# A parallel Hedgehog-attention and gMLP block: a later GELU, sixteen loads of wo, remainders split in place, and block stores on GpSimd's queue

## The chip, the core and the metric

The kernel runs on one core of one Trainium2 chip. The metric is device time in microseconds (us), median of three runs; beside it there is one profiled execution, whose trace gives the time of every instruction on TensorE (PE, with its weight loads as PEld), VectorE (DVE), ScalarE (ACT), GpSimd (POOL) and SyncE (SP, which here only issues DMAs). SPq, POOLq and ACTq are the queues of these engines.

## The reference

x has 2048 tokens of 512 features. After one layer norm, two branches are added to x: linear attention with a learned double softmax over 32 heads, and a gMLP whose spatial gate mixes all 2048 tokens.

```python
xn = _layernorm(x, axis=-1)
return x + _A_ref(xn, A_wqkv, A_w_phi, A_wo) + _B_ref(xn, B_w_in, B_w_sp, B_b_sp, B_w_out)

# attention branch: feature map, sums over tokens, projection by wo
phi_q = concat(softmax(pq), softmax(-pq));  phi_k = concat(softmax(pk), softmax(-pk))
kv = einsum("bhsf,bhsd->bhfd", phi_k, v);   z = einsum("bhsf->bhf", phi_k)
o = einsum("bhqf,bhfd->bhqd", phi_q, kv) / (einsum("bhqf,bhf->bhq", phi_q, z)[..., None] + 1e-6)
return o.transpose(...).reshape(B, S, D) @ wo

# gMLP branch: 688 + 688 features, spatial product over tokens
z = gelu(x @ w_in);  z1 = z[..., :Fh];  z2 = layernorm(z[..., Fh:])
g = einsum("ts,bsf->btf", w_sp, z2) + b_sp[None, :, None]
return (z1 * g) @ w_out
```

All matrices are float32.

## The kernel before

Tokens are cut into 16 tiles of 128 rows. A float32 product is made of three TensorE products of rounded parts: a matrix is split into its rounded part and the rest, by a copy on ACT (`round_h`, L45) and a subtraction on DVE (`rest_l`, L49), and `mm3` (L51) multiplies high by high, high by low and low by high.

The program has four stages. From 0 to about 225 us the tokens are normalised, turned and projected; z1 (the first 688 features of the gMLP, before GELU) and the attention's exponentials go out to DRAM (`z1_d`, `e_d`). From there to about 290 us z2 is projected, normalised and split into the operands B. Then comes the **spatial stage**, to about 506 us, and last the **output stage**, which multiplies the gated tiles by w_out and the attention's output by wo and adds x.

The spatial stage works on pairs of token tiles, i = 0 to 7 (`NP` is 8). For a pair, `products` runs over four groups of source tokens (`NQ` is 4; n counts the 32 groups of the stage). One group is 7 block products (`FORM`, a form of Strassen's) of 6 matmuls, so a pair is 168 matmuls into seven PSUM tiles g. Two groups ahead, `prep_a` makes the operands A for group n + 2: sums S on DVE, and for each of four pieces a rounding on ACT and a subtraction on DVE. `load_a` loads the raw weights `wf` three groups ahead on SP's queue.

At the end of a pair, `drain` adds up the seven PSUM tiles into the tile c (first the ACT copy of L711, then seven DVE additions, L710 to L715), and `gate` does the rest: GELU on ACT over `z1t`, the product of GELU and c on DVE (L727), the split of the 48 remainder columns into a rounded part and a rest (L730, L49, L732; 688 is five times 128 plus 48), and a transpose in blocks of 32 on DVE (L733), which writes its result **back into `z1t`**. Four stores then carry `z1t` to `u_d` in DRAM, 32 partitions each, in runs of 32 elements (128 bytes): 32 x 46 = 1472 runs a store. `z1t` and `c` have one buffer each, so the next pair's `load_z1` (two loads on POOL's queue) waits until the four stores have landed, and GELU waits for that load. Before, the stores stand on SP's queue among the loads of `wf`; those of pair 6 are held back behind the loads `et`.

A scheduler turns program order into the order of each engine. It places instructions by an estimate of its own; `tc.issue_after(ins)` ties those inside it behind `ins` on the same engine. `gate` ties GELU behind the first drain copy. Within an engine the order is then fixed: whoever waits holds up all behind it.

In the output stage, tiles u come back from `u_d` (`fetch_u`: five blocks u and the 96 remainder rows rt), are split, and are multiplied by w_out (`project_u`). `attend_T` and `attend` turn the attention's features and multiply them by kv into the tile po; oT is its split form, and `project_o` multiplies oT by wo. wo itself is loaded at the start of this stage: four loads of 128 rows, whose source pattern takes 32 rows from each of four places, each followed by a split into woh and wol. The tiles er are copies of finished features made by DMA on POOL's queue. The gate of pair 7 runs in the middle of this stage (after tile 8), with its own stores from `zt`.

Of the kernel before, what the change touches and what calls it, by code (L numbers as in the profile page):

```python
# [10 lines left out]
F32 = mybir.dt.float32  # L11
F32R = mybir.dt.float32r
# [6 lines left out]
P = 128  # L19
S, D, H, DH, FH = 2048, 512, 32, 16, 688  # L20
# [4 lines left out]
NF = 2 * D  # L25
KF = FH // P
REM = FH - KF * P
FU = FH + REM
BL = 32
# [3 lines left out]
NP = NT // 2  # L33
HP, QP = P // 2, P // 4
# [3 lines left out]
def mixer(ctx: ExitStack, tc: tile.TileContext, x, x_t, wv, wqkT, phi_bd, wo, w_in, wst, b_r, w_out, out):  # L38
    nc = tc.nc
    pe, act, dve, pool, sp = nc.tensor, nc.scalar, nc.vector, nc.gpsimd, nc.sync  # L40


    def round_h(eng, h, src):
        if eng is act:
            return act.activation(h, src, AF.Copy).ins  # L45
        return eng.tensor_copy(h, src).ins

    def rest_l(l, src, h, eng=None):
        return (eng or dve).tensor_tensor(l, src, h.bitcast(F32), op=ALU.subtract).ins  # L49
# [19 lines left out]
    e_d = dram.tile([NT, P, NF + 2 * H], F32, name="e_d")  # L69
# [96 lines left out]
    with ExitStack() as p0:  # L166
# [71 lines left out]
        xt, v, rounded, ready = {}, {}, [], []  # L238
# [131 lines left out]
        t = xz.tile([P, 2, FH], F32R, tag="xz", name="xT")  # L370
        xT.append(t)
        x0, pts = xt.pop(0), []
        for k in range(2):
            pts.append(ps.tile([P, 2, P], F32, tag="mm", name="pt"))
            for c in range(2):
                i = pe.transpose(pts[k][:, c], x0[:, (2 * k + c) * P:(2 * k + c + 1) * P], ident).ins
            keep(pe=i)
        warm_up(2)
        for cs, pt in zip(halves, pts):
            src = pt.rearrange("p a b -> p (a b)")  # L380
            i = round_h(act, t[:, 0, cs], src)
# [7 lines left out]
        p = ps.tile([P, D], F32, tag="mm", name="proj")  # L389
# [7 lines left out]
        p = ps.tile([P, D], F32, tag="mm", name="proj")  # L397
# [18 lines left out]
        p = ps.tile([P, D], F32, tag="mm", name="proj")  # L416
# [60 lines left out]
    QW = NF + 7 * H  # L477

    def load_q(s, et):
        load_q.last = sp.dma_start(et[:, :NF + 2 * H], e_d[s]).ins  # L480
        return et

    def q_fin(et, tmp, zb):
# [13 lines left out]
    NQ = NT // QC  # L497
# [3 lines left out]
    SEQ = [(i, q) for i in range(NP) for q in (range(NQ) if i < NP - 1 else (1, 2, 3, 0))]  # L501

    def b_parts(h, l, src):
        round_h(act, h, src)
        rest_l(l, src, h)

    def load_a(n):
        i, q = SEQ[n]
        f = []
        for k in range(2):  # L510
            t = ws.tile([P, QC, P], F32, tag=f"f{k}", bufs=2, name="wf")
            sp.dma_start(t, wst[2 * i + k, :, q * QC:(q + 1) * QC, :])
            f.append(t.rearrange("p (k two) t -> p two k t", two=2))
        return f

    def prep_a(n, f):

        a, b = f
        pl = hl[n % 2]
        ops = {}  # L520

        def parts(names, src):
            t = pl.tile([P, 2, len(names), 2, P], F32R, tag="".join(names), name="A")
            b_parts(t[:, 0], t[:, 1], src)
            for k, m in enumerate(names):
                ops[m] = t[:, 0, k], t[:, 1, k]

        sums = ws.tile([P, 4, 2, P], F32, tag="S", name="S")
        parts(("A11", "A12"), a)
        dve.tensor_tensor(sums[:, 0], b[:, 0], b[:, 1], op=ALU.add)  # L530
        dve.tensor_tensor(sums[:, 1], sums[:, 0], a[:, 0], op=ALU.subtract)  # L531
        parts(("S1", "S2"), sums[:, 0:2])
        dve.tensor_tensor(sums[:, 2], a[:, 0], b[:, 0], op=ALU.subtract)
        dve.tensor_tensor(sums[:, 3], a[:, 1], sums[:, 1], op=ALU.subtract)
        parts(("S3", "S4"), sums[:, 2:4])
        parts(("A22",), b[:, 1:2])
        return ops
# [3 lines left out]
    with ExitStack() as p1:  # L541
# [45 lines left out]
        for s in range(NE):  # L587
            et = load_q(s, tb.tile([P, QW], F32, tag="et", bufs=2, name="et"))
# [58 lines left out]
    for s in range(NT):  # L647
        p = zproj((kv_ps_p, zc, zbp, za)[s % 4], s, w2, (0, 1) if s % 2 == 0 else (1, 0))
        n = s // 2
        if s % 2 == 0:  # L650
            z2[n] = zw.tile([P, 4, FC], F32, tag="z2", bufs=2, name="z2")
        z = z2[n][:, 2 * (s % 2):2 * (s % 2) + 2]
# [8 lines left out]
        r = zw.tile([P, 1], F32, tag="rstd", bufs=2, name="rstd")  # L661
# [23 lines left out]
    gt = mid.enter_context(right("gt", 1))  # L685
# [20 lines left out]
    def drain(i, g, cb):  # L706
        g = {k: t[:, :FC] for k, t in g.items()}
        b1, b2 = (bias[:, 2 * i + k:2 * i + k + 1] for k in range(2))
        c11, c12, c21, c22 = (cb[:, k, j] for k in range(2) for j in range(2))
        add = lambda o, p, b, q: dve.scalar_tensor_tensor(o, p, b, q, op0=ALU.add, op1=ALU.add)  # L710
        first = act.activation(c12, g["P1"], AF.Copy)  # L711
        add(c11, g["P2"], b1, c12)
        dve.tensor_tensor(c21, g["P6"], c12, op=ALU.add)
        dve.tensor_tensor(c12, g["P5"], c21, op=ALU.add)
        dve.tensor_tensor(c21, g["P7"], c21, op=ALU.add)  # L715
        add(c22, g["P5"], b2, c21)
        add(c12, g["P3"], b1, c12)
        drained = add(c21, g["P4"], b2, c21)
        return cb, first.ins, drained.ins

    def gate(i, cb, z, u, ut):
        cb, first, _ = cb
        with tc.issue_after(first):
            act.activation(z[:, :, :FH], z[:, :, :FH], AF.Gelu_apprx_tanh)
        zs = z[:, :, :FH].rearrange("p k (j f) -> p k j f", j=2)
        us = u[:, :, :FH].rearrange("p k (j f) -> p k j f", j=2)
        dve.tensor_tensor(us, zs, cb, op=ALU.mult)  # L727
        rm = slice(KF * P, FH)
        rh = gt.tile([P, 2, REM], F32R, tag="rh", name="rh")
        dve.tensor_copy(rh, u[:, :, rm])  # L730
        rest_l(u[:, :, FH:FH + REM], u[:, :, rm], rh)
        dve.tensor_copy(u[:, :, rm], rh.bitcast(F32))  # L732
        dve.transpose(ut.rearrange("p k f -> p (k f)"), u.rearrange("p k f -> p (k f)"))  # L733

        def store():
            src = ut.rearrange("p k f -> p (k f)")
            dst = u_d[2 * i:2 * i + 2].rearrange("k (j a) t -> a (k j) t", a=BL)
            for b in range(0, P, BL):
                sp.dma_start(dst[:, :, b:b + BL], src[b:b + BL].rearrange("p (m b) -> p m b", b=BL))

        return store

# [3 lines left out]
    def load_w(src, parts, h, l, t):  # L746
        rows = 0
        for r0, r1 in parts:
            sp.dma_start(t[rows:rows + r1 - r0], src[r0:r1, :])
            rows += r1 - r0  # L750
        return round_h(act, h, t[:rows]), rest_l(l, t[:rows], h)
# [37 lines left out]
    g, es, ets = {}, {}, {}  # L789
    for n in range(NC):  # L790
        i = SEQ[n][0]
        if n % NQ == 1 and i < NP - 1:
            z = load_z1(i)
        products(n, g)
        if n % NQ == NQ - 1 and i < NP - 1:
            c = gt.tile([P, 2, FU], F32, tag="c", name="c")
            cq = c[:, :, :FH].rearrange("p k (j f) -> p k j f", j=2)
            store = gate(i, drain(i, g, cq), z, c, z)
            if i < NP - 2:
                store()  # L800
            g = {}
        if n + 3 < NC:
            raw[n + 3] = load_a(n + 3)
        if n + 2 < NC:
            A[n + 2] = prep_a(n + 2, raw.pop(n + 2))
        if n == NC - 4:
            stage_w()
        if n == NC - 3:
            zs = slot("zb", F32R)
            zb, ident_r = zs[:, :NF].bitcast(F32), zs[:, NF:NF + P]  # L810
            round_h(act, ident_r, ident)
            sp.dma_start(zb, zb_d)
            uT = [first_gate(0)]
            es[0], es[1] = first_q(0), first_q(1)
        if n == NC - 2:
            t = slot("u1", F32R)
            us = {1: load_u(1, k_tiles(t[:, :KF * P]).bitcast(F32), t[:2 * REM, KF * P:(KF + 1) * P])}
            ets[2], ets[3] = (load_q(s, slot("et")) for s in (2, 3))
            with tc.issue_after(load_q.last):
                store()  # L820
    cb = drain(NP - 1, g, slot("c").rearrange("p (k j f) -> p k j f", k=2, j=2))
    with tc.issue_after(cb[1]), tc.issue_after(cb[2]):
        es[2], last = q_fin(ets.pop(2), slot("qtmp")[:, :NF], zb)
# [4 lines left out]
    gt = p2.enter_context(right("gl", 1))  # L828
    cw = ctx.enter_context(left("cw", 1))
# [3 lines left out]
    def fetch_u(i):  # L833
        return load_u(i, cw.tile([P, KF, P], F32, tag="u", bufs=4, name="u"),
                      cw.tile([2 * REM, P], F32R, tag="rt", bufs=6, name="rt"))
# [82 lines left out]

    GATE_LAST = 8

    for s in (2, 3):
        us[s] = fetch_u(s)
    wo_h, wo_l = (cw.tile([P, ND, D], F32R, name=f"wo{k}") for k in "hl")
    p = {0: project_u(0, uT.pop(0))}
    fT = attend_T(0)
    with tc.issue_after(lasts[5]), tc.issue_after(lasts[1]), tc.issue_after(fin[-1]):
        for c in range(ND):
            t = cw.tile([P, D], F32, tag="wof", bufs=4, name="wof")
            sp.dma_start(t, wo.rearrange("(k m a r) d -> k a m r d", k=2, a=2, r=QP)[c // 2, c % 2])
            round_h(act, wo_h[:, c], t)  # L930
            rest_l(wo_l[:, c], t, wo_h[:, c])
    p[1] = project_u(1, uT.pop(0))
    oT, ins = attend(fT)
    fin.append(ins)
# [10 lines left out]
    for i in range(0, NT, 2):  # L945
# [15 lines left out]
        if i == 2:  # L961
            with tc.issue_after(lasts[6]):
                z = load_z1(NP - 1)
# [40 lines left out]
```

## Time and profile before

| what | value |
|---|---|
| median of 3 runs (lowest, highest) | 653.47 us (652.96, 654.95) |
| the profiled execution's own time | 652.16 us |
| its span in the trace | 650.4 us |
| mean granted TensorE clock | 0.987 of full speed |
| DVE, ACT, POOL busy | 80%, 41%, 13% of the span |
| DMA packets under 512 B | 52208 of 94725 |
| HBM read, written | 56.37 MB, 26.61 MB |

Busy shares are means over stages that are limited by different things. What an edit is worth is read in its own stage, from the engine that ends last there and from what released it; the profile names for each idle time the instruction that ended it.

### The profile page before, as it was taken

What the parts mean: (1) busy time and instruction counts of PE and PEld (TensorE: products, weight loads), DVE (VectorE), ACT (ScalarE), POOL (GpSimd) and SP (SyncE); (2) the same over time, 40 slices, a digit from 0 to 9 for tenths busy, and PEclk for the clock granted to TensorE, in tenths of its full rate; (3) what the DMA queues carried; (4) which work ended last, traced back from release to release, by engine and by line L of the source; (5) the groups of instructions that cost most, each with busy time, mean ns of one, the idle gap of its engine ahead of it and who ended that gap; (6) DMA issues with size and microseconds to landing.
All of it is one profiled execution on the core that took longest, in us unless ns stands there. A gap on an engine that the chain in (4) does not pass through costs nothing.

```text
span 650.4 us, 11408 instructions
## 1 busy us (share of the span) xinstructions
PE 627.9 (97%) x4406; PEld 569.9 (88%) x4406; DVE 518.4 (80%) x916; ACT 269.0 (41%) x431; POOL 86.2 (13%) x168
## 2 busy tenths in 40 slices
PE   8999999999999999999999998998999769999998
PEld 6888888888889999999999898998999657777776
DVE  5999979987977699899969678595968569899822
ACT  5643434433324558785343233343335222323220
POOL 4143212111011034440000000000000000100000
PEclk9999999999999999999999998999899969999999
DMA  8345554444356920014455363735559768986921
GB/s 326 141 98 139 134 159 140 112 133 124 88 156 185 324 91 1 2 34 136 102 140 108 129 147 99 163 83 142 104 169 292 174 203 278 316 275 226 248 97 36
DMA packets 94725, 98.39 MB, mean 151 GB/s; under 512 B 52208, under 2 KB 65264, under 8 KB 94672
## 3 DMA queue, kind: packets, MB, share of 16 engines
q1 hardware_dynamic: 84752, 62.81, 34.8%
q0 software_dynamic: 7616, 29.23, 15.2%
q10 hardware_dynamic: 2304, 5.64, 2.3%
q8 instruction: 34, 0.56, 0.3%
q14 instruction: 19, 0.16, 0.1%
HBM read 56.37 MB, written 26.61 MB: 128 GB/s over the span
## 4 chain that ended last, share of the span: by engine, by line
PE 86%; DMA 7%; DVE 3%; issue 2%; SPq 1%; ACT 1%; POOL 0%; ACTq 0%; POOLq 0%; DVEq 0%
PE g L53 9%; PE g L55 9%; PE g L54 9%; PE proj L55 7%; PE proj L53 7%; PE proj L54 7%; PE zps L55 6%; PE zps L53 6%; PE zps L54 6%; PE pout L53 4%; PE pout L54 4%; PE pout L55 4%; DMA wof<-in_wo 2%; DMA z1t<-z_d 2%; DMA et<-e_d 1%
## 5 line engine op out<-in xcount | busy, mean ns | idle before, releaser
L53 PE MATMUL g<-B,A 128*128 128x344 f32 x448 | 145.0, 324 | 6.6 <-DVE c L715 6.6
L54 PE MATMUL g<-B,A 128*128 128x344 f32 x448 | 144.6, 323 | 0.0
L55 PE MATMUL g<-B,A 128*128 128x344 f32 x448 | 144.2, 323 | 0.0
L53 PEld LDWEIGHTS g<-B,A 128*128 128x128 f32 x448 | 85.3, 190 | 8.0 <-DVE c L715 8.0
L54 PEld LDWEIGHTS g<-B,A 128*128 128x128 f32 x448 | 85.3, 190 | 0.0
L55 PEld LDWEIGHTS g<-B,A 128*128 128x128 f32 x448 | 85.3, 190 | 0.0
L45 ACT ACTIVATE A<-S 128x512 fp32r<-128x512 f32 x64 | 39.4, 627 | 70.7 <-DVE S L531 53.0
L49 DVE TENSOR_TENSOR A<-wf,A 128x512 fp32r<-128x512 f32 x64 | 35.4, 554 | 22.8 <-ACT A L45 22.5
L113 ACT ACTIVATE e<-e,r_x 128x1024 f32<-128x1024 f32 x28 | 32.2, 1150 | 49.9 <-DVE e L112 49.9
L53 PE MATMUL proj<-wqk_h,xT 128*128 128x512 f32 x128 | 50.9, 398 | 0.0
L55 PE MATMUL proj<-wqk_h,xT 128*128 128x512 f32 x128 | 50.6, 395 | 0.0
L54 PE MATMUL proj<-wqk_l,xT 128*128 128x512 f32 x128 | 50.3, 393 | 0.0
L49 DVE TENSOR_TENSOR A<-S,A 128x512 fp32r<-128x512 f32 x64 | 43.9, 687 | 7.2 <-ACT A L45 7.0
L53 PE MATMUL zps<-w_0h,xT 128*128 128x344 f32 x128 | 41.4, 323 | 0.0
L55 PE MATMUL zps<-w_0h,xT 128*128 128x344 f32 x128 | 41.1, 321 | 0.0
L53 PE MATMUL zps<-w_1h,xT 128*128 128x344 f32 x128 | 41.0, 320 | 0.0
L55 PE MATMUL zps<-w_1h,xT 128*128 128x344 f32 x128 | 40.9, 320 | 0.0
L54 PE MATMUL zps<-w_0l,xT 128*128 128x344 f32 x128 | 40.9, 319 | 0.0
L54 PE MATMUL zps<-w_1l,xT 128*128 128x344 f32 x128 | 40.9, 319 | 0.0
L45 ACT ACTIVATE A<-wf 128x512 fp32r<-128x512 f32 x64 | 31.8, 514 | 15.3 <-issue 7.2
L116 DVE TENSOR_REDUCE sm<-e 128x64 f32<-128x1024 f32 x28 | 33.9, 1211 | 4.9 <-ACT e L113 4.8
L53 PE MATMUL pout<-woh,oT 128*128 128x512 f32 x60 | 24.6, 410 | 9.9 <-ACT oT L45 9.9
(208 smaller groups left out, 1400.2 us busy)
## 6 DMA issues: line engine op xcount, KB each, us to landing
wf<-in_wst SPq DMA_DIRECT2D x64, 256.0 KB, 3.8
e_d<-e POOLq DMA_DIRECT2D x16, 544.0 KB, 5.2
et<-e_d SPq DMA_DIRECT2D x16, 544.0 KB, 5.5
zacc<-e POOLq DMA_DIRECT2D x12, 512.0 KB, 4.7
er<-et POOLq DMA_DIRECT2D x12, 512.0 KB, 4.9
z_d<-z1f ACTq DMA_DIRECT2D x16, 344.0 KB, 2.2
z1t<-z_d POOLq DMA_DIRECT2D x16, 344.0 KB, 6.0
u_d<-z1t SPq DMA_DIRECT2D x28, 184.0 KB, 4.5
```

The lines of the kernel that those rows point to most:

```text
L45: return act.activation(h, src, AF.Copy).ins
L49: return (eng or dve).tensor_tensor(l, src, h.bitcast(F32), op=ALU.subtract).ins
L53: pe.matmul(dst, ah, bh, start=start, stop=False)
L54: pe.matmul(dst, ah, bl, start=False, stop=False)
L55: return pe.matmul(dst, al, bh, start=False, stop=stop).ins
L113: act.activation(e, e, AF.Exp, scale=scale)
L116: dve.tensor_reduce(sm, heads(e), axis=AX.X, op=ALU.add)
```

## The change

Four edits. GELU of pairs 0 to 6 is tied behind the last rounding of the `prep_a` that follows the drain (`prep_a.last`, from `b_parts`), and `gate` is called after that `prep_a`. The remainders are split in place: the rounded part is cast into the spare columns and the rest overwrites the source, so the tile rh and the copy of L732 go, and rounded part and rest change places in `u_d`; the products with w_out take both rows alike. All block stores to `u_d`, those of pair 7 too, are issued by POOL, and the hold on pair 6's stores goes. wo is loaded by `load_w`, in four loads of 32 rows for each of four tiles, and stands ahead of `fetch_u` for tiles 2 and 3.

```diff
     def load_q(s, et):
-        load_q.last = sp.dma_start(et[:, :NF + 2 * H], e_d[s]).ins
+        sp.dma_start(et[:, :NF + 2 * H], e_d[s])
         return et
...
     def b_parts(h, l, src):
-        round_h(act, h, src)
+        rounded = round_h(act, h, src)
         rest_l(l, src, h)
+        return rounded
...
-            b_parts(t[:, 0], t[:, 1], src)
+            prep_a.last = b_parts(t[:, 0], t[:, 1], src)
...
-    def gate(i, cb, z, u, ut):
+    def gate(i, cb, z, u, ut, after=None):
         cb, first, _ = cb
-        with tc.issue_after(first):
+        with tc.issue_after(after or first):
             act.activation(z[:, :, :FH], z[:, :, :FH], AF.Gelu_apprx_tanh)
...
         dve.tensor_tensor(us, zs, cb, op=ALU.mult)
-        rm = slice(KF * P, FH)
-        rh = gt.tile([P, 2, REM], F32R, tag="rh", name="rh")
-        dve.tensor_copy(rh, u[:, :, rm])
-        rest_l(u[:, :, FH:FH + REM], u[:, :, rm], rh)
-        dve.tensor_copy(u[:, :, rm], rh.bitcast(F32))
+        lo, hi = u[:, :, KF * P:FH], u[:, :, FH:FU].bitcast(F32R)
+        dve.tensor_copy(hi, lo)
+        rest_l(lo, lo, hi)
         dve.transpose(ut.rearrange("p k f -> p (k f)"), u.rearrange("p k f -> p (k f)"))
...
             for b in range(0, P, BL):
-                sp.dma_start(dst[:, :, b:b + BL], src[b:b + BL].rearrange("p (m b) -> p m b", b=BL))
+                pool.dma_start(dst[:, :, b:b + BL], src[b:b + BL].rearrange("p (m b) -> p m b", b=BL))
...
-            store = gate(i, drain(i, g, cq), z, c, z)
-            if i < NP - 2:
-                store()
+            cb = drain(i, g, cq)
             g = {}
         if n + 3 < NC:
             raw[n + 3] = load_a(n + 3)
         if n + 2 < NC:
             A[n + 2] = prep_a(n + 2, raw.pop(n + 2))
+        if n % NQ == NQ - 1 and i < NP - 1:
+            gate(i, cb, z, c, z, prep_a.last)()
...
             ets[2], ets[3] = (load_q(s, slot("et")) for s in (2, 3))
-            with tc.issue_after(load_q.last):
-                store()
...
-    for s in (2, 3):
-        us[s] = fetch_u(s)
     wo_h, wo_l = (cw.tile([P, ND, D], F32R, name=f"wo{k}") for k in "hl")
...
         for c in range(ND):
-            t = cw.tile([P, D], F32, tag="wof", bufs=4, name="wof")
-            sp.dma_start(t, wo.rearrange("(k m a r) d -> k a m r d", k=2, a=2, r=QP)[c // 2, c % 2])
-            round_h(act, wo_h[:, c], t)
-            rest_l(wo_l[:, c], t, wo_h[:, c])
+            rows = [(m * QP, (m + 1) * QP) for m in range(c // 2 * 8 + c % 2, (c // 2 + 1) * 8, 2)]
+            load_w(wo, rows, wo_h[:, c], wo_l[:, c], cw.tile([P, D], F32, tag="wof", bufs=4, name="wof"))
+    for s in (2, 3):
+        us[s] = fetch_u(s)
```

**ACT at the end of pair 5.** c is the drained tile, g its PSUM products, A and S the operands of the next groups. Before:

```order
L711 ACTIVATE c_4946<-g_4705 128x344
L724 ACTIVATE z1t_4775<-z1t_4775 128x2x688
L45 ACTIVATE A_4971<-wf_4883 128x512
L45 ACTIVATE A_4976<-S_4970 128x512
L45 ACTIVATE A_4981<-S_4970 128x512
L45 ACTIVATE A_4984<-wf_4885 128x256
```

And changed:

```order
L712 ACTIVATE c_4936<-g_4695 128x344
L45 ACTIVATE A_4950<-wf_4873 128x512
L45 ACTIVATE A_4955<-S_4949 128x512
L45 ACTIVATE A_4960<-S_4949 128x512
L45 ACTIVATE A_4963<-wf_4875 128x256
L725 ACTIVATE z1t_4765<-z1t_4765 128x2x688
```

GELU went from ahead of the four roundings to behind them. The same holds for pairs 1 to 6; in pair 0 GELU stood behind three of the roundings already.

**POOL's queue in the spatial stage.** Each u_d row is four stores. Before, from the end of the stage ahead, where POOL still made the tiles nb:

```order
L664 TENSOR_SCALAR nb_3220<-mv_3215,rstd_3216 128x1
L692 DMA z1t_3365<-z1_d_64 128x688 x2
L692 DMA z1t_3647<-z1_d_64 128x688 x2
L692 DMA z1t_3929<-z1_d_64 128x688 x2
L692 DMA z1t_4211<-z1_d_64 128x688 x2
```

And changed:

```order
L693 DMA z1t_3365<-z1_d_64 128x688 x2
L738 DMA u_d_65<-z1t_3365 32x46x32 x4
L693 DMA z1t_3645<-z1_d_64 128x688 x2
L738 DMA u_d_65<-z1t_3645 32x46x32 x4
L693 DMA z1t_3925<-z1_d_64 128x688 x2
L738 DMA u_d_65<-z1t_3925 32x46x32 x4
```

The four stores of a pair now stand on the queue of the two loads that wait for them.

**SP's queue at the start of the output stage.** u and rt are the gated tiles and their remainder rows. Before:

```order
L480 DMA et<-e_d 128x1088 x2
L739 DMA u_d<-z1t 32x46x32 x4
L855 DMA kvT<-kvT_d 128x512
L754 DMA u<-u_d 128x5x128
L755 DMA rt<-u_d 96x128
L754 DMA u<-u_d 128x5x128
L755 DMA rt<-u_d 96x128
L929 DMA wof<-in_wo 128x1x512 x4
L905 DMA xr<-in_x 128x512
```

And changed:

```order
L480 DMA et<-e_d 128x1088 x2
L852 DMA kvT<-kvT_d 128x512
L748 DMA wof<-in_wo 32x512 x16
L753 DMA u<-u_d 128x5x128
L754 DMA rt<-u_d 96x128
L753 DMA u<-u_d 128x5x128
L754 DMA rt<-u_d 96x128
L902 DMA xr<-in_x 128x512
```

The loads of wo moved ahead of two pairs of u and rt and became sixteen; pair 6's stores left the queue. On ACT, the four roundings of wo are still followed by the split of u, now of two tiles u instead of one, and only then by the two roundings of oT.

## The prediction

> **What bounds the kernel now.** I read the engines' busy line first, then what TensorE waited for. The wait rows give who waited, on whom, us in total, times, longest.
>
> ```profile
> PE 627.9 (97%) x4406; PEld 569.9 (88%) x4406; DVE 518.4 (80%) x916; ACT 269.0 (41%) x431; POOL 86.2 (13%) x168
> PE pout L53 <- ACT oT L45: 9.9, 1, 9.9
> PE g L53 <- DVE c L715: 6.6, 4, 2.7
> ```
>
> TensorE sets the time: it is idle for 650.4 - 627.9 = 22.5 us, and two kinds of waits make 16.5 of them: four waits in the spatial stage, and one at the start of the output stage. To price the first kind I cut the stage at the starts of the drain copy L711 (first and last of eight shown), which follow TensorE's progress, and read the stretches between; columns are length, busy us of PE, PEld, DVE, ACT, POOL, and the granted clock.
>
> ```profile
> 304.68 0.46 ACT L711 ACTIVATE c<-g 128x344 f32<-128x344 f32 x1 [0.48 <-PE g L55]
> 500.81 0.46 ACT L711 ACTIVATE c<-g 128x344 f32<-128x344 f32 x1 [1.49 <-PE g L55]
> 304.68:331.15 26.47, 26.47 (x170) 26.47 (x169) 24.22 (x51) 11.60 (x20) 1.06 (x2) 1.00 0.59 144
> 331.15:357.58 26.43, 26.43 (x170) 26.43 (x169) 21.27 (x44) 10.30 (x18) 0.02 (x1) 1.00 0.49 117
> 357.58:385.64 28.06, 26.71 (x170) 26.42 (x169) 21.27 (x44) 10.08 (x18) 1.04 (x2) 1.00 0.48 122
> 385.64:415.70 30.06, 28.25 (x170) 27.96 (x169) 21.37 (x44) 10.19 (x19) 2.09 (x4) 0.94 0.57 132
> 415.70:443.17 27.47, 26.70 (x170) 26.42 (x169) 21.27 (x44) 10.06 (x18) 0.03 (x1) 1.00 0.49 116
> 443.17:474.08 30.91, 28.23 (x170) 27.95 (x169) 21.36 (x44) 10.18 (x19) 1.97 (x4) 0.94 0.55 129
> 474.08:500.81 26.73, 26.73 (x170) 26.48 (x169) 21.68 (x43) 11.94 (x22) 0.15 (x1) 1.00 0.71 224
> ```
>
> All seven hold the same 170 matmuls. Two run without a gap, in 26.45; the others are longer by 1.6, 3.6, 1.0, 4.5 and 0.3, **11.0 us in all**: more than the 6.6 of waiting, since the clock falls to 0.94 after the longer gaps. The third stretch shows the cause, on ACT and DVE.
>
> ```profile
> 364.24 1.35 ACT L724 ACTIVATE z1t<-z1t 128x1376 f32<-128x1376 f32 x1 [6.20 <-DMA z1t<-z_d]
> 365.50 0.61 ACT L45 ACTIVATE A<-wf 128x512 fp32r<-128x512 f32 x1
> 361.52 0.51 DVE L713 TENSOR_TENSOR c<-g,c 128x344 f32<-128x344 f32 x1
> 366.15 0.69 DVE L49 TENSOR_TENSOR A<-wf,A 128x512 fp32r<-128x512 f32 x1 [4.12 <-ACT A L45]
> 367.78 0.51 DVE L715 TENSOR_TENSOR c<-g,c 128x344 f32<-128x344 f32 x1
> ```
>
> GELU waits 6.2 us for its input from DRAM. Behind it on ACT stands a rounding of A; DVE waits 4.1 for that in the middle of its drain; so L715, which frees a PSUM tile, comes late, and TensorE waits for it. A late load reaches TensorE through two queues with which it has nothing to do.
>
> **GELU later.** Behind the roundings it holds up neither the drain nor A for group n + 2. It is queued ahead of the roundings for group n + 3, and the product L727 waits for it on DVE. How late may it be? Pair 0 already had nearly that order, and ran without a gap:
>
> ```profile
> 307.89 1.36 ACT L724 ACTIVATE z1t<-z1t 128x1376 f32<-128x1376 f32 x1
> 314.77 1.58 DVE L727 TENSOR_TENSOR c<-z1t,c 128x1376 f32<-128x1376 f32 x1
> 342.42 1.59 DVE L727 TENSOR_TENSOR c<-z1t,c 128x1376 f32<-128x1376 f32 x1
> 347.91 1.71 DVE L733 STREAM_TRANSPOSE z1t<-c 128x1472 f32<-128x1472 f32 x1
> 349.64 3.97 SPq L739 DMA_DIRECT2D u_d<-z1t  x4
> 357.56 1.06 POOL L692 DMA_DIRECT2D z1t<-z_d  x2 [28.02 <-DVE A L49]
> ```
>
> There GELU began 3.2 us after the drain copy and DVE reached L727 10.1 after it, so a start up to 10.1 - 1.4 = 8.7 after costs nothing. Beyond that DVE idles, and it has 26.45 - 21.3 = 5.1 us a pair to spare: TensorE is hit from a lateness of about 13. All of the 11.0 goes if GELU stays earlier than that. I book 10, and leave 1 for waits on the weight loads.
>
> **Stores on POOL.** They decide whether it stays earlier, for z1t goes round: GELU 1.35, from L727 to the end of the transpose 349.62 - 342.42 = 7.2, the stores, the loads, GELU. The stores take 7.9 us now (349.62 to 357.56): 3.97 to issue and 4.0 until the last has landed. From the loads' issue to GELU it is 364.24 - 357.56 = 6.7. With G for POOL's time on four stores, a round is 1.35 + 7.2 + G + 4.0 + 6.7 = 19.25 + G, against 26.45 a pair. **Up to G = 7.2 the loop is free**; beyond, GELU falls behind by G - 7.2 a pair, and with 13 - 3 = 10 us of room over six rounds the cost is 6 (G - 7.2) - 10. SP, freed of these stores, issues weight loads with nothing between. What is G? Groups of POOL's transfers (mean ns after the comma, then idle), and SP's issues (min/median/max ns):
>
> ```profile
> L692 POOL DMA_DIRECT2D z1t<-z_d x16 | 8.6, 545 | 177.4 <-ACT A L45 55.2 <-DMA u_d<-z1t 28.5 <-DVE A L49 28.0
> L845 POOL DMA_DIRECT2D er<-et x12 | 6.4, 531 | 133.5 <-DMA xr<-in_x 66.0 <-DVE et L494 47.6 <-PE ptq L870 7.9
> L301 POOL DMA_DIRECT2D zacc<-e x12 | 10.9, 912 | 73.2 <-DVE e L300 35.1 <-DVE e L117 27.8 <-ACT v L281 7.9
> L739 SPq DMA_DIRECT2D u_d<-z1t x28: 325/888/3074, 320.7 to 504.5; - x28
> L512 SPq DMA_DIRECT2D wf<-in_wst x64: 327/328/2420, 205.0 to 485.8; - x64
> ```
>
> No POOL transfer of this trace has the form of a store: they have 128 long runs, a store has 1472 short ones. Lower bound: runs cost nothing, 4 x 0.545 = 2.2 us. Upper bound: all in proportion, 0.545 x 1472 / 128 = 6.3 a store, 25 us. Between: the accumulating transfer takes 0.38 us more than the plain one; if that were a second reading of its 128 runs, a run would cost 3.0 ns, a store 0.53 + 1344 x 3.0 ns = 4.6, four of them 18. For the low side: rows of 2752 and of 4096 bytes take alike (545 and 531), and on SP a store's 1472 runs can be issued as fast (325 ns) as a weight load's 128 (327). I take the geometric middle of the two bounds, 1.85 us a store, **G = 7.4**: a price of zero.
>
> The Trainium skill (DMA: Bandwidth & Descriptors, "Anatomy of one DMA — SWDGE (gpsimd) path") calls descriptor generation small and variable, and says that many can be emitted before the cost shows; by it G is near 2.2 and the sum is the same. No run here shows it.
>
> **Remainders in place.** One DVE copy of 0.2 us a pair goes, below DVE's spare 5.1: zero. If DVE were the bound it would be 8 x 0.2 = 1.6 us.
>
> **wo.** The wait at the start of the output stage:
>
> ```profile
> 506.01 1.41 SPq L855 DMA_DIRECT2D kvT<-kvT_d  x1
> 509.60 2.76 SPq L929 DMA_DIRECT2D wof<-in_wo  x4
> 524.83 0.63 ACT L45 ACTIVATE woh<-wof 128x512 fp32r<-128x512 f32 x1 [2.57 <-DMA wof<-in_wo]
> 515.65 1.09 PE L885 MATMUL po<-f,kvT 64*32 64x256 f32 x32
> 526.62 0.79 PE L53 MATMUL pout<-woh,oT 128*128 128x512 f32 x1 [9.87 <-ACT oT L45]
> wof<-in_w_out SPq DMA_DIRECT2D x5, 256.0 KB, 4.1
> u<-u_d SPq DMA_DIRECT2D x15, 320.0 KB, 4.6
> L749 SPq DMA_DIRECT2D wof<-in_w_out x7: 376/423/913, 482.4 to 488.6; - x7
> ```
>
> TensorE ends its own work at 516.7. The fourth load of wo, issued by 512.4, lets ACT go on at 524.8, some 12.5 us later, where the plain loads of w_out land in 4.1. ACT rounds it, then u, then oT, for which TensorE waits until 526.6. Now: the loads start at 507.4, behind kvT; sixteen issues at the median 0.42 take 6.8, to 514.2; the last lands at 518.3. But the loads of two pairs u and rt are behind them: four issues at 0.42, to 515.9, landing at 520.5, and ACT rounds both tiles u before oT: 0.6 each for the second u and oT, like woh, so TensorE goes on at about 521.7. **Gain 4.9, booked as 4.5.** Bounds: 9.9 if nothing is left of the wait; a loss of 3 if every issue took the longest 0.91 (8 us later than counted).
>
> **Pair 7's gate** puts its four stores ahead of three copies er on POOL. Of these the first is needed soonest:
>
> ```profile
> 600.78 1.70 DVE L733 STREAM_TRANSPOSE zt<-z1t 128x1472 f32<-128x1472 f32 x1
> 615.11 1.32 PE ptq L870 x16
> ```
>
> With the stores begun at 602.5 and G = 7.4, it is issued at 609.9 and, with 0.5 and a landing like that of u, is there at 615.0; and DVE now reaches the transpose two instructions sooner. Zero; G - 7.5 where G is larger.
>
> **Sum**, against the profiled execution (span 650.4, its own time 652.16): 652.2 - 10 - 4.5 = 637.7. The median of the runs lies 1.3 above that execution, so I forecast **639**. What follows the two gains is bound by TensorE and moves up with it.
>
> **Rivals.**
>
> *POOL becomes the bound (slower).* Each store's runs are worked off one by one on POOL, z1t comes back too late, ACT and DVE stand behind GELU and L727, and TensorE starves for A in pairs 2 to 7. It decides from where 6 (G - 7.2) - 10 eats the 14.5: G = 11.3, or **2.8 us a store**. At G = 18 the stage loses 54.8 and pair 7's gate 10.5: 652.2 - 14.5 + 65.3 + 1.3 = 704; at 14 they are 30.8 and 6.5, which makes 676; at 25, 753. For it: 1472 runs against 128, and the accumulating row. Against it: the equal rows for different bytes, and SP's issue. POOL could also be held up by DVE, which is busy for 21.3 of 26.45; but in the first stage transfers took 0.64 and 0.91 us on the mean beside a DVE as busy (107.6 of 130 us):
>
> ```profile
> L295 POOL DMA_DIRECT2D e_d<-e x16 | 10.2, 640 | 26.0 <-DVE e L117 9.6 <-DVE zl L49 4.5 <-issue 3.8
> 100.00:230.00 130.00, 130.00 (x1035) 115.03 (x1034) 107.60 (x161) 51.14 (x74) 15.91 (x25) 1.00 0.54 161
> ```
>
> The Trainium skill (SBUF — State Buffer, "Who interferes with whom") says that only copies, casts and scalar operations in a two-port mode shut POOL out while descriptors are written; here that would be the cast of 0.2 us a pair. By it this second cause is worth nothing.
>
> *The change does not do what it says (about no change).* With G from about 10.5 to 12, GELU is tied later but its input comes later too, and what the order gains the stores give back: 648 to 656.
>
> *The wait for wo only changes its owner.* oT now waits for u in place of wo, and sixteen issues run at the slow end: 652.2 - 10 + 3 + 1.3 = 646, still faster. For it: 32-row loads were never issued in this trace.
>
> **How the numbers follow.** Forecast (with the third rival as its slow side) 0.60, its own range 630 to 649; POOL as the bound 0.32; give and take 0.08, a quarter of it faster than 0.3%, half within, a quarter slower. A measurement of this kernel can tell about 0.3% (2 us) from no change: faster 0.62, within 0.04, slower 0.34. The range runs from 630 (all 11.0, all 9.9, and some of the clock: 1 in 20 below) to 688, which holds six tenths of the slow case: about 0.14 above.
>
> **What would show it.** Right: stretches between drain copies of 26.5 us with the clock at 1.00; GELU no more than 9 us after the drain copy; u_d stores on POOL below 2 us each; the wait on oT near 5 us. Wrong: stores above 2.8 us on POOL, GELU waiting on z1t for longer from pair to pair, DVE idle ahead of L728; or a wait on oT that stays near 10, with u as its last releaser.

## The result, and the profile after

| kernel | median of runs, us | lowest to highest | profiled execution | its span |
|---|---|---|---|---|
| before | 653.22 (4 runs) | 652.86 to 654.95 | 652.16 | 650.4 |
| changed | 634.27 (4 runs) | 632.42 to 635.17 | 635.06 | 633.3 |

The ratio is 0.9701, with a 95% interval of 0.9671 to 0.9732: faster, by 19 us. The forecast was 639.

The engines' busy line of the changed kernel, and its waits (who waits for whom, us in total, times, longest):

```profile
PE 624.5 (99%) x4406; PEld 567.9 (90%) x4406; DVE 520.1 (82%) x908; ACT 273.9 (43%) x431; POOL 115.0 (18%) x200
```

```profile
PE pout L53 <- ACT oT L45: 2.6, 1, 2.6
POOL z1t L693 <- DMA u_d<-z1t: 34.6, 5, 7.2
```

TensorE's four waits for the drain (6.6 us) are gone, and the wait at the start of the output stage fell from 9.9 to 2.6. The stage, cut at the drain copies again (now L712; columns as in the prediction):

```profile
305.20:331.67 26.47, 26.47 (x170) 26.47 (x169) 23.92 (x50) 11.47 (x21) 3.64 (x4) 1.00 0.56 150
...
384.53:410.97 26.44, 26.44 (x170) 26.44 (x169) 21.78 (x44) 11.08 (x19) 4.11 (x5) 1.00 0.51 134
...
463.83:490.85 27.02, 27.02 (x173) 27.02 (x172) 20.85 (x41) 12.70 (x22) 3.63 (x4) 1.00 0.73 210
```

The seven stretches now sum to 490.85 - 305.20 = 185.65 us in place of 196.13: **10.5 us** from the stage. The clock is at 1.00 throughout; in no stretch is TensorE idle.

One round of z1t in the changed kernel, that of pair 1, as a timeline (start, duration; in brackets the idle time of the engine ahead and what ended it):

```profile
331.67 0.46 ACT L712 ACTIVATE c<-g 128x344 f32<-128x344 f32 x1 [0.53 <-PE g L55]
338.06 1.36 ACT L725 ACTIVATE z1t<-z1t 128x1376 f32<-128x1376 f32 x1 [0.30 <-DMA z1t<-z_d]
339.47 1.58 DVE L728 TENSOR_TENSOR c<-z1t,c 128x1376 f32<-128x1376 f32 x1
344.32 1.71 DVE L732 STREAM_TRANSPOSE z1t<-c 128x1472 f32<-128x1472 f32 x1
346.60 3.63 POOL L738 DMA_DIRECT2D u_d<-z1t  x4 [12.85 <-ACT A L45]
356.69 1.12 POOL L693 DMA_DIRECT2D z1t<-z_d  x2 [6.46 <-DMA u_d<-z1t]
```

GELU starts 6.4 us after the drain copy, DVE takes its product up at once, and the stores go out 8.5 us after GELU's start. Four stores hold POOL for 3.63 us, and the next loads follow 10.1 us after the first store. GELU waits for z1t 0.3 us here and in no other pair; before, it waited in six of seven.

The output stage's start, as a timeline of SP's queue, ACT and TensorE:

```profile
490.34 0.32 SPq L852 DMA_DIRECT2D kvT<-kvT_d  x1
493.60 8.55 SPq L748 DMA_DIRECT2D wof<-in_wo  x16
502.16 2.34 ACT L45 ACTIVATE woh<-wof 128x512 fp32r<-128x512 f32 x4
507.59 0.74 ACT L45 ACTIVATE uh<-u 128x640 fp32r<-128x640 f32 x1 [1.11 <-DMA u<-u_d]
508.23 1.07 ACT L45 ACTIVATE oT<-po 128x512 fp32r<-128x512 f32 x2
508.86 0.80 PE L53 MATMUL pout<-woh,oT 128*128 128x512 f32 x1 [2.62 <-ACT oT L45]
```

oT starts 17.4 us after the last drain copy (508.23 - 490.85), where it was 25.2 before: **7.8 us** more. The owner of what is left is u. The stage's 10.5 and these 7.8 make 18.3; the span fell by 17.1, so 1.2 us came back elsewhere, in parts too small to name. (The last stretch above holds 173 matmuls and not 170: its drain copy was taken up some 0.5 us late. So about 0.5 of the 7.8 belongs to the stage, and the wait alone fell by 7.3.)

### The profile page after: what moved, and what is told of

It reads as the page before. It is cut to its first block, busy times and chain, and to the rows that moved or that the text cites. A ratio compares the mean times of both kernels' runs of the same rounds, so it can differ in the third digit from the quotient of the medians.

```text
span 633.3 us, 11447 instructions
## 1 busy us (share of the span) xinstructions
PE 624.5 (99%) x4406; PEld 567.9 (90%) x4406; DVE 520.1 (82%) x908; ACT 273.9 (43%) x431; POOL 115.0 (18%) x200
## 3 DMA queue, kind: packets, MB, share of 16 engines
q0 software_dynamic: 9664, 35.26, 22.4%
## 4 chain that ended last, share of the span: by engine, by line
PE 95%; DMA 3%; SPq 1%; issue 0%; ACT 0%; DVE 0%; ACTq 0%
PE g L55 11%; PE g L54 11%; PE g L53 11%; PE proj L55 7%; PE proj L53 7%; PE proj L54 7%; PE zps L55 6%; PE zps L53 6%; PE zps L54 6%; PE pout L53 5%; PE pout L54 5%; PE pout L55 5%; PE ptq L867 1%; PE kvps L312 1%; DMA kvT<-kvT_d 1%; PE po L882 1%
## 5 line engine op out<-in xcount | busy, mean ns | idle before, releaser
L54 PE MATMUL g<-B,A 128*128 128x344 f32 x448 | 143.2, 320 | 0.0
L53 PE MATMUL g<-B,A 128*128 128x344 f32 x448 | 143.1, 319 | 0.0
L55 PE MATMUL g<-B,A 128*128 128x344 f32 x448 | 142.9, 320 | 0.0
L53 PEld LDWEIGHTS g<-B,A 128*128 128x128 f32 x448 | 84.2, 188 | 0.0
L55 PEld LDWEIGHTS g<-B,A 128*128 128x128 f32 x448 | 84.1, 188 | 0.0
L54 PEld LDWEIGHTS g<-B,A 128*128 128x128 f32 x448 | 84.1, 188 | 0.0
L45 ACT ACTIVATE A<-wf 128x512 fp32r<-128x512 f32 x64 | 33.4, 522 | 38.6 <-PE g L55 29.2
L738 POOL DMA_DIRECT2D u_d<-z1t x28 | 25.4, 914 | 104.7 <-ACT A L45 42.4
```

What stands on the lines that cost most here:

```text
L53: pe.matmul(dst, ah, bh, start=start, stop=False)
L54: pe.matmul(dst, ah, bl, start=False, stop=False)
L55: return pe.matmul(dst, al, bh, start=False, stop=stop).ins
L738: pool.dma_start(dst[:, :, b:b + BL], src[b:b + BL].rearrange("p (m b) -> p m b", b=BL))
```

## The experiments

Each kernel is set beside runs of the kernel before on the same chip, whose median lay between 652.0 and 652.5 (653.22 for the changed kernel). "Stage" is the time from the first drain copy to the last of pairs 0 to 7; "wait" is TensorE's wait on the first oT. Both are read from one profiled execution a kernel; those of stores_only (653.50 us) and oT_first (638.22) were the slowest of their runs, 3 us above the median.

| run | what it is | median, us | ratio, 95% interval | stage | wait |
|---|---|---|---|---|---|
| (before) | | | 1 | 196.1 | 9.9 |
| (changed) | all four edits | 634.27 | 0.9701, 0.9671 to 0.9732 | 185.7 | 2.6 |
| gelu_only | before + GELU later | 642.63 | 0.9850, 0.9827 to 0.9873 | 185.1 | 12.0 |
| stores_only | before + stores on POOL, no hold | 650.46 | 0.9965, 0.9945 to 0.9984 | 197.6 | 9.1 |
| rem_only | before + split in place | 644.41 | 0.9877, 0.9848 to 0.9905 | 187.8 | 10.7 |
| wo_sixteen | before + 16 loads of wo, old place | 645.83 | 0.9914, 0.9883 to 0.9945 | 194.6 | 4.5 |
| gelu_early | changed, GELU back | 640.91 | 0.9823, 0.9793 to 0.9853 | 189.9 | 3.7 |
| stores_sp | changed, stores back on SP, no hold | 636.79 | 0.9759, 0.9739 to 0.9780 | 187.4 | 6.2 |
| rem_old | changed, old split | 633.87 | 0.9721, 0.9705 to 0.9737 | 185.1 | 3.3 |
| wo_four | changed, 4 loads of wo | 638.74 | 0.9788, 0.9763 to 0.9812 | 186.1 | 6.1 |
| wo_behind_u | changed, wo behind u again | 633.43 | 0.9712, 0.9687 to 0.9737 | 185.7 | 2.4 |
| stores_x2 | changed, stores twice | 654.44 | 1.0026, 1.0008 to 1.0045 | 196.0 | 8.0 |
| stores_x3 | changed, stores three times | 701.90 | 1.0759, 1.0740 to 1.0777 | 227.9 | 18.4 |
| oT_first | changed, oT ahead of u on ACT | 635.27 | 0.9745, 0.9713 to 0.9776 | 185.5 | 0.7 |

### GELU's place alone

```diff
+            cb = drain(i, g, cq)
...
+        if n % NQ == NQ - 1 and i < NP - 1:
+            store = gate(i, cb, z, c, z, prep_a.last)
+            if i < NP - 2:
+                store()
```

> The kernel before with one edit: GELU tied behind the last rounding of the prep_a that follows the drain; stores stay on SP's queue, pair 6's held back as before. Theory (the gain of the stage is GELU's place): the store loop on SP is no longer than on POOL (7.9 us from transpose to the next loads against some 10), so GELU starts 6 to 9 us after the drain copy, the seven stretches sum to 185 to 186 us in place of 196, TensorE's 6.6 us of waits for the drain go, wo is as before: 642 to 644 us. Rival (the gain came from taking the stores off SP's queue): the stretches stay uneven and the time stays at 652 to 654.

The stage of this kernel in one stretch, and its wait on oT:

```profile
304.98:490.09 185.11, 185.11 (x1178) 185.11 (x1177) 155.01 (x313) 79.06 (x133) 6.38 (x12) 1.00 0.58 149
```

```profile
PE pout L53 <- ACT oT L45: 12.0, 1, 12.0
```

All 11.0 us of the stage go with this edit alone, with the stores on SP and the old split. The rival falls: POOL's stores are not what the stage gains from. The wait on oT grew by 2.1 us. The loads of wo start 9.1 us after the last drain copy there, where it was 8.8 before; the rest of the 2.1 is not explained.

### The stores alone, and GELU put back

```diff
-                sp.dma_start(dst[:, :, b:b + BL], src[b:b + BL].rearrange("p (m b) -> p m b", b=BL))
+                pool.dma_start(dst[:, :, b:b + BL], src[b:b + BL].rearrange("p (m b) -> p m b", b=BL))
```

> The kernel before with one edit: all block stores on POOL's queue and no hold on pair 6; GELU stays ahead of the roundings. Theory: the loop from transpose to loads grows by some 2 us (10.1 against 7.9), so GELU waits for z1t longer than the 34.6 us of before and the stage gains nothing or loses up to 2 us a pair (0 to +10 us); the loads of wo start earlier because kvT no longer stands behind pair 6's stores, worth 3 to 5 us: 648 to 659. Rival (the stores on POOL are the gain of the stage): the seven stretches come to 26.5 us each and the time to 638 to 640.

```diff
             cb = drain(i, g, cq)
+            gate(i, cb, z, c, z)()
             g = {}
...
-            gate(i, cb, z, c, z, prep_a.last)()
```

> The changed kernel with GELU tied behind the first drain copy again, ahead of the roundings; all else as changed. Theory: the stage's 10.5 us are lost again, with up to 2 us a pair more because the stores take longer to land on POOL's queue, while the output stage keeps its 7.3 us: 644 to 656, with waits of TensorE for the drain's additions. Rival (GELU's place is worth nothing once the stores are on POOL): 634 to 636.

With the stores alone (the hold on pair 6's stores goes too) the stage is 1.5 us longer and the wait on oT 0.8 shorter, in an execution 3 us above the median. The stage moved by as much in wo_sixteen, which has no edit there, so the 1.5 is no sure loss; but it is no gain of 10, so the rival falls. The runs lie between 647.8 and 653.5, and more than a small gain can't be read from them. With GELU put back in the changed kernel only 4.2 of the 10.5 us are lost, although the stores land no sooner: less than the theory said. In the stage the two kernels differ by the split of the remainders alone, yet their stages are 7.7 us apart. So that split had a price which the theory lacked.

### The split of the remainders

```diff
-        rm = slice(KF * P, FH)
-        rh = gt.tile([P, 2, REM], F32R, tag="rh", name="rh")
...
+        lo, hi = u[:, :, KF * P:FH], u[:, :, FH:FU].bitcast(F32R)
+        dve.tensor_copy(hi, lo)
+        rest_l(lo, lo, hi)
```

> The kernel before with one edit: the remainders split in place (the tile rh and the copy of it go). Theory of the prediction: DVE has 5 us a pair to spare, so nothing: 652 to 654. Rival, from the two runs with GELU early (the changed kernel's GELU put back came to 640.9, the kernel before with stores on POOL to 650.5, and only the remainders differ in their stage): two instructions fewer move the transpose ahead in DVE's order, the loop of z1t is 1 to 1.5 us shorter a round and GELU waits less, 3 to 8 us in the stage: 644 to 650.

The run went the rival's way. The main reason is in the round of z1t. The kernel before, from GELU of pair 2 (at 364.24, shown in the prediction) to GELU of pair 3:

```profile
371.26 1.58 DVE L727 TENSOR_TENSOR c<-z1t,c 128x1376 f32<-128x1376 f32 x1
376.76 1.71 DVE L733 STREAM_TRANSPOSE z1t<-c 128x1472 f32<-128x1472 f32 x1
386.31 1.06 POOL L692 DMA_DIRECT2D z1t<-z_d  x2 [27.68 <-ACT c L711]
392.76 1.35 ACT L724 ACTIVATE z1t<-z1t 128x1376 f32<-128x1376 f32 x1 [6.66 <-DMA z1t<-z_d]
```

The split in place alone, from GELU of pair 3 to GELU of pair 4:

```profile
390.19 1.36 ACT L724 ACTIVATE z1t<-z1t 128x1376 f32<-128x1376 f32 x1 [1.12 <-DMA z1t<-z_d]
397.21 1.58 DVE L727 TENSOR_TENSOR c<-z1t,c 128x1376 f32<-128x1376 f32 x1
401.58 1.70 DVE L731 STREAM_TRANSPOSE z1t<-c 128x1472 f32<-128x1472 f32 x1
403.31 3.87 SPq L737 DMA_DIRECT2D u_d<-z1t  x4
411.03 1.07 POOL L692 DMA_DIRECT2D z1t<-z_d  x2 [26.06 <-DMA u_d<-z1t]
417.03 1.36 ACT L724 ACTIVATE z1t<-z1t 128x1376 f32<-128x1376 f32 x1 [0.44 <-issue]
```

Before, a round took 392.76 - 364.24 = 28.5 us, longer than TensorE's 26.45 (27.5 to 29.4 over the six rounds): **z1t's loop paced the stage**. Of it 7.0 us lay between GELU's start and L727, since the roundings behind GELU on ACT hold the drain's additions, which stand ahead of L727 on DVE. From there to the transpose's end it was 7.2, then 7.8 to the loads and 6.5 to the next GELU. With the split in place the copy of L732 (0.20 us) is gone, and in DVE's order the transpose now stands ahead of a subtraction for A and two instructions for S (0.42 us each) that stood ahead of it before: L727 to the transpose's end takes 401.58 + 1.70 - 397.21 = 6.1. A round is then 26.8 us (26.7 to 28.0 over the six), from pair 2 on GELU waits at most 1.1 us for z1t, and the stage is 8.4 us shorter. From the loads to GELU it is 6.0 us there, 0.5 less than before, which the edit does not explain.

The edit moved more than DVE's order. The scheduler also put the stores one load of wf earlier on SP's queue, and the drain copies of pairs 2 to 6 start about 4 us later against TensorE, which in the second stretch had done 27 matmuls of the next pair (columns as in the prediction):

```profile
331.23:361.92 30.69, 30.69 (x197) 30.69 (x196) 20.30 (x42) 9.64 (x18) 1.07 (x2) 1.00 0.50 130
```

How much of the 7.6 us this shift gives or takes was not tested.

```diff
-        lo, hi = u[:, :, KF * P:FH], u[:, :, FH:FU].bitcast(F32R)
...
+        rm = slice(KF * P, FH)
+        rh = gt.tile([P, 2, REM], F32R, tag="rh", name="rh")
```

> The changed kernel with the remainders split as before (tile rh and the copy of it back). Theory: in place of the old split, only the loop of z1t and the scheduler's order gain, and with GELU behind the roundings both are covered: 634 to 635, the wait for the drain stays at nothing. Rival (the split is worth the 7.6 us that it gave alone to the kernel before): 638 to 642.

In the changed kernel the old split costs nothing that can be told: 0.9721 and 0.9701 have intervals that overlap, and the stage is 185.1. GELU behind the roundings already takes the loop from 28.5 us to below 26.45 (GELU to L728 is 1.4 in place of 7.0). The two edits cure one illness, so their gains don't add: the four edits tried alone (three here, wo below) sum to 9.9 + 2.1 + 7.6 + 6.2 = 25.8 us, together they give 19.

### The stores back on SP

```diff
-                pool.dma_start(dst[:, :, b:b + BL], src[b:b + BL].rearrange("p (m b) -> p m b", b=BL))
+                sp.dma_start(dst[:, :, b:b + BL], src[b:b + BL].rearrange("p (m b) -> p m b", b=BL))
```

> The changed kernel with the stores on SP's queue, without a hold on pair 6's. Theory: the stage keeps its stretches of 26.5 us, since the loop is shorter on SP; pair 6's four stores stand ahead of the loads et and kvT again, and of pair 0's and pair 1's loads u, wait for the transpose some 15 us after the drain copy, and push the loads of wo back by 0 to 10 us: the wait on oT is 3 to 10 us in place of 2.6, 634 to 642. POOL's busy time falls back by about 29 us and the count of packets rises from 49 thousand to about 94 thousand. Rival (SP's issue of stores among the weight loads costs the stage): stretches above 27 us, 640 to 650.

TensorE has no gap in the stage here either; its 187.4 comes from drain copies that ACT took up late, the last one behind a rounding that waited for u. What is lost is in the output stage: the wait is 6.2 in place of 2.6. The loads of wo start no later than in the changed kernel (493.60 there), but take 12.0 us to issue in place of 8.55:

```profile
493.18 11.99 SPq L748 DMA_DIRECT2D wof<-in_wo  x16
```

So it is the end of the hold, and not POOL's queue, that lets them start early. The stores' move is worth 0.6% by the ratios and 2.5 us by the medians in the changed kernel, and not through the stage; why the sixteen issues are slower is not shown.

### POOL's time on the stores, doubled and trebled

```diff
+            for to in [u_d] + (u_x if i < NP - 1 else []):
+                dst = to[2 * i:2 * i + 2].rearrange("k (j a) t -> a (k j) t", a=BL)
...
+                    pool.dma_start(dst[:, :, b:b + BL], src[b:b + BL].rearrange("p (m b) -> p m b", b=BL))
```

> The changed kernel that stores each gated tile of pairs 0 to 6 a second time on POOL's queue, to a DRAM tensor that nothing reads: G = 7.3 us in place of 3.64. The prediction's rule (free to G = 7.2, then 6 (G - 7.2) - 10): nothing, 634 to 635. The same rule with the rows of the changed kernel (GELU to stores 8.5, G, 6.7 to the loads, 5 from the loads to GELU, 26.45 a pair): free to 6.25, the first stores lie late, so GELU starts 10 us after the drain copy in pair 1 and some 15 in pair 6: 634 to 638. Rival (POOL's time on stores never decides, only GELU's place in the order): 634 to 635 here and with three times the stores.

> As the run with stores twice, but three times: G = 10.9 us. The prediction's rule: 6 x 3.7 - 10 = 12, 646. With the rows of the changed kernel: pair 1's GELU starts 13.7 us after the drain copy and falls back by 4.7 a pair, so that some 24 us reach TensorE: 646 to 662, with waits of GELU on z1t and of TensorE on A or on the drain. Rival (POOL's time on stores never decides): 634 to 636.

Both were costlier than any theory said: 654 against at most 638, and 702 against at most 662. Doubled, from GELU of pair 2 to GELU of pair 3 (u_x is the second tensor):

```profile
376.31 1.35 ACT L726 ACTIVATE z1t<-z1t 128x1376 f32<-128x1376 f32 x1 [5.81 <-DMA z1t<-z_d]
384.12 3.63 POOL L740 DMA_DIRECT2D u_d<-z1t  x4 [12.83 <-DVE A L49]
387.74 3.58 POOL L740 DMA_DIRECT2D u_x<-z1t  x4
401.35 1.12 POOL L694 DMA_DIRECT2D z1t<-z_d  x2 [10.03 <-DMA wf<-in_wst]
405.83 1.35 ACT L726 ACTIVATE z1t<-z1t 128x1376 f32<-128x1376 f32 x1 [7.76 <-DMA z1t<-z_d]
```

```profile
u_d<-z1t POOLq DMA_DIRECT2D x28, 184.0 KB, 6.0
u_x<-z1t POOLq DMA_DIRECT2D x28, 184.0 KB, 9.3
```

POOL's time is as expected, 3.6 us for each four. But the loads follow 10.0 us after the last issue, and the second tensor's stores land in 9.3 us, not 6.0. (The row at 401.35 names a load of wf as what ended POOL's wait; in three of the other five rounds it is the stores to u_x, after 9.4 to 10.7 us.) From the first store to the loads it is 10.1 us for four stores (changed), 17.2 for eight, and 382.34 - 358.85 = 23.5 for twelve, here with the trebled run from GELU of pair 1 to GELU of pair 2:

```profile
350.83 1.36 ACT L726 ACTIVATE z1t<-z1t 128x1376 f32<-128x1376 f32 x1 [2.41 <-DMA z1t<-z_d]
358.85 3.62 POOL L740 DMA_DIRECT2D u_d<-z1t  x4 [12.42 <-DVE S L536]
...
382.34 1.12 POOL L694 DMA_DIRECT2D z1t<-z_d  x2 [11.97 <-DMA u_x<-z1t]
387.12 1.36 ACT L726 ACTIVATE z1t<-z1t 128x1376 f32<-128x1376 f32 x1 [5.73 <-DMA z1t<-z_d]
```

So four more cost 6.3 to 7.1 us, 1.6 to 1.8 a store, against 0.91 of issue: their landing paces them, not POOL's own time. A round is 405.83 - 376.31 = 29.5 us doubled (28.0 to 34.1 over the six); trebled it is 387.12 - 350.83 = 36.3 (35.7 to 44.2). Of the 20 us that the doubled stores cost, 10.3 are in the stage and 5.4 in the wait on oT; the rest is not traced. The loop becomes the bound between four and eight stores a pair: a round of the changed kernel without waits is 8.5 + 10.1 + 4.5 = 23.1, so the stores have some 3.3 us to spare (4.5 is from the loads to GELU in the doubled run).

### wo

```diff
-            sp.dma_start(t, wo.rearrange("(k m a r) d -> k a m r d", k=2, a=2, r=QP)[c // 2, c % 2])
...
+            rows = [(m * QP, (m + 1) * QP) for m in range(c // 2 * 8 + c % 2, (c // 2 + 1) * 8, 2)]
+            load_w(wo, rows, wo_h[:, c], wo_l[:, c], cw.tile([P, D], F32, tag="wof", bufs=4, name="wof"))
```

> The kernel before with one edit: wo loaded in sixteen loads of 32 rows, still behind the loads of two pairs u and rt, with pair 6's stores ahead on SP. Theory (the pattern of the four loads costs, their landing of some 12 us): the loads start at about 509.6 as before, sixteen issues take 8.5 us, the last lands 2.2 to 4 us later, oT is ready at 521.5 to 523 in place of 526.6: the wait on oT is 5 to 6.5 us in place of 9.9, 648 to 650. Rival (only the place in the queue and SP's being free count): wait and time as before, 652 to 654.

The reverse in the changed kernel is the run wo_four:

> The changed kernel with wo in four loads of 128 rows, each gathered from four places, at the new place ahead of u. Theory: the fourth is issued about 3 us after the first and lands some 12 us later, so oT comes 2 to 6 us later than in the changed kernel: wait on oT 4.5 to 8 us, 636 to 640. Rival (the four loads were late only because SP and the rings were full of pair 6's stores): 634 to 635, with a landing near 3 us.

```diff
+    for s in (2, 3):
+        us[s] = fetch_u(s)
     wo_h, wo_l = (cw.tile([P, ND, D], F32R, name=f"wo{k}") for k in "hl")
```

> The changed kernel with the loads of tiles 2 and 3 (u and rt) back ahead of the sixteen loads of wo. Theory: oT waits for u there, not for wo, so wo loses 2 us of start and u gains: the wait on oT stays between 1.5 and 4 us, 633 to 636. Rival (wo's place ahead of u is what gains): the wait rises by 3 us or more, 637 and above.

The pattern counts, the place does not. Sixteen loads at the old place bring the wait from 9.9 to 4.5 us; the place ahead of u brings nothing (2.4 with wo behind u, 2.6 ahead, though behind u its loads start 6.85 us after the last drain copy and ahead of it 2.75). With four loads at the new place, and SP's queue free, the wait is 6.1:

```profile
493.14 2.87 SPq L924 DMA_DIRECT2D wof<-in_wo  x4
504.91 0.63 ACT L45 ACTIVATE woh<-wof 128x512 fp32r<-128x512 f32 x1 [2.04 <-DMA wof<-in_wo]
508.58 0.63 ACT L45 ACTIVATE woh<-wof 128x512 fp32r<-128x512 f32 x1 [3.04 <-DMA wof<-in_wo]
```

The fourth load, issued by 496.0, is there 12.6 us later, as it was before the change (12.5). The last two come 3.7 us apart for 256 KB each, while sixteen loads of 64 KB were all issued in 8.55 us and each landed in a median of 2.2 (changed kernel: source, count, KB each, median us to landing).

```profile
wof<-in_wo SPq DMA_DIRECT2D x16, 64.0 KB, 2.2
```

So it was neither SP's queue nor pair 6's stores that made the four slow.

The Trainium skill (DMA: Bandwidth & Descriptors, "Why a DMA increments its semaphore by 16 and not by 1") says that a copy runs on the largest number of DMA engines, up to 16, that divides the sizes of both sides' slowest dimension: that makes 4 for a source of four places, and 16 for 32 rows. The times agree with it in direction; no run here shows the engines that a load used.

### oT ahead of the splits of u

```diff
-            round_h(act, oT[0][:, qs], po[r])
+            attend.last = round_h(act, oT[0][:, qs], po[r])
...
+            with tc.issue_after(attend.last):
+                nxt[2], nxt[3] = gated(us.pop(2)), gated(us.pop(3))
```

> The changed kernel with one edit in the output stage: the splits of u for tiles 2 and 3 are tied behind the roundings of the first oT. Theory (oT now waits on ACT for two roundings that wait for u): oT starts when po is done, at about 506.5 in place of 508.2, the wait of TensorE falls from 2.6 to about 1 us, and u is needed only 13 us later: 632 to 633. Rival (the splits of u are then late for tile 2's product, or DVE's half of oT is the last): 634 to 636, with a new wait of TensorE on uh.

TensorE's waits in this run:

```profile
PE ptq L867 <- DMA er<-et: 2.3, 1, 2.3
PE pout L53 <- DVE xr L913: 1.7, 2, 1.1
PE pout L53 <- ACT oT L45: 0.7, 1, 0.7
```

The wait on oT went as expected. The profiled execution, 3 us slower than the median, shows other waits in its place, for er and xr; whether the faster runs have them is not known. The time is not lower. No version tried is told from the changed kernel as faster: wo_behind_u and rem_old lie within its interval.

## Why the prediction was right, and where it was not

**GELU later: 10 booked, 10.5 in the stage.** The mechanism holds: GELU's edit alone frees the whole stage, and in the changed kernel GELU starts 6.0 to 6.4 us after the drain copy, under the 8.7 that was named free. What failed is how the loop was counted. "A round is 1.35 + 7.2 + G + 4.0 + 6.7" took GELU to L727 at 1.35 us; by that sum the old loop (with SP's 7.9) would have been 23.2 and free. It was 28.5, because with GELU first the step is 7.0. The prediction saw a late load passing through two queues; it did not see that those queues stood inside the loop which made the load late.

**Stores on POOL: free to G = 7.2, taken 7.4.** G is 3.63: 0.914 us a store, nearer the lower bound (0.545) than the geometric middle (1.85). The groups of POOL's stores and loads:

```profile
L738 POOL DMA_DIRECT2D u_d<-z1t x28 | 25.4, 914 | 104.7 <-ACT A L45 42.4 <-DVE A L49 32.5 <-DVE S L531 29.9
...
L693 POOL DMA_DIRECT2D z1t<-z_d x16 | 9.0, 566 | 54.3 <-DMA u_d<-z1t 34.6 <-issue 13.3 <-DMA wf<-in_wst 6.4
```

The Trainium skill (DMA: Bandwidth & Descriptors, "Anatomy of one DMA — SWDGE (gpsimd) path"), which was cited for small generation costs, agrees with this row.

The forecast of nothing in the stage came true, but not by the price it was given. The loop's term "4.0 until the last has landed", taken from SP, is 6.5 on POOL's queue, and grows to 10 with eight stores. In the changed kernel the prediction's sum still comes out, 22.9 against 23.1, because the loads reach GELU sooner: 4.5 us in place of 6.7, as far as the doubled run shows it. That the cost of more stores is 6 (G - 7.2) - 10 is refuted: it gave nothing for the doubled ones, which cost 20 us, and 12 for the trebled ones, which cost 68. The doubled run has G = 7.2, about what the forecast took, and nothing of the gain is left in it. It moves twice the bytes as well, so four slow stores might have cost less; but that the forecast held is owed to a G of half the size taken, and this was in good part **luck**, though the prediction had named rows that spoke for the low side.

**Remainders: zero.** Right in the changed kernel (rem_old), wrong as argued. "Below DVE's spare 5.1" asked only for DVE's busy time; alone the edit gave 7.6 us, with a shorter loop and another order on DVE. (One instruction a pair goes, 916 to 908 on DVE, where the prediction's paragraph on pair 7's gate and the expectation of rem_only say two.)

**wo: 4.5 booked, 7.8 measured.** The owner changed to u, as predicted, and the sixteen loads issue at 0.53 us each, a little above the median taken. Mis-sized was their start: 507.4, 6.6 us after the last drain copy, put kvT where it stood before. But kvT had stood behind pair 6's stores, held back on SP; with these gone the loads start 2.75 us after the last drain copy (493.60 - 490.85), 3.8 us sooner than counted. The slower issue took 1.7 of that back (8.55 in place of 6.8), and oT's other steps were shorter than counted. The sixteen loads alone, with the stores held back on SP as before (wo_sixteen), cut the wait by 5.4 at the old place, of the size worked out (4.9); the end of the hold was read from the order and not booked.

**Pair 7's gate: zero**, as predicted: its four stores took 3.63 us, and TensorE shows no wait for er.

**The sum.** 639 less the measured 634.3 is 4.7: the stage gave 0.5 more, wo 3.3 more, 1.2 came back elsewhere, and the median lies 0.8 below the profiled execution where 1.3 above was assumed (2.1).

**The rivals.** POOL as the bound did not come about; the doubled stores show how near it was, by landing and not by POOL's own time. "About no change" was put at a G of 10.5 to 12; the doubled stores came to it at 7.2. Nor was POOL held up by DVE: the 28 stores took 902 to 947 ns each, beside a DVE busy for 21.8 of 26.4 us.

```profile
L738 POOL DMA_DIRECT2D u_d<-z1t x28: 902/913/947, 321.8 to 481.5; - x28
```

The wait for wo did change its owner, but on a shorter wait.

## What to carry to other kernels

Where one buffer goes round through several engines and DRAM, add up the whole round, with what stands ahead of each step in its queue, and compare it with the time of the engine that should set the pace; an edit off the bottleneck that shortens such a loop is worth at most what it takes off a round, times the rounds, until the round is as short as that engine's time; a second edit that shortens the same loop is then worth nothing more. When a group of DMAs leaves its place in a queue, book also what moves up behind it. Price stores in a loop by when they land, not by how long the issuing engine is busy.

## What the hardware showed unexpectedly

The same 32 block stores make 2048 packets on POOL's queue and 47104 on SP's. The packet count of stores_only, which moves nothing but the stores:

```profile
DMA packets 49158, 98.40 MB, mean 151 GB/s; under 512 B 5104, under 2 KB 18160, under 8 KB 49104
```

Before, 52208 packets were under 512 B: 47104 more, which is 32 x 1472, one for each run of 128 bytes. In the changed kernel POOL's queue carries 9664 packets where it was 7616: 2048, or 64 a store, each 188416 / 64 = 2944 bytes, 23 runs. Fewer packets did not land sooner. Changed, and then before:

```profile
u_d<-z1t POOLq DMA_DIRECT2D x28, 184.0 KB, 5.9
```

```profile
u_d<-z1t SPq DMA_DIRECT2D x28, 184.0 KB, 4.5
```

The median is 5.9 us on POOL's queue and 4.5 on SP's, and from the first of four stores to the loads it is 10.1 against 7.9 in the rounds shown.

In these traces POOL's time hardly grows with the runs: 0.914 us for 1472 of them and 0.566 for a load of 128, which would be 0.26 ns a run if the runs make the difference.
